# Tails of q and k of two batches: two transfers over 128 partitions in place of four over 64, turned by matmuls with every second identity group, and another set of planning constants

## Chip, core, metric

One core of a Trainium2 chip runs the whole program. The metric is device time in microseconds, the median of several executions. A profile is one further execution, with its own time.

## What is computed

Sliding-window attention for 8 batches of 8 heads, 576 tokens, head dimension 64 (a token attends to keys at most 32 positions away), and behind it a two-layer feed-forward net on the 4608 tokens. Inputs and output are float32; the kernel multiplies in bfloat16.

```python
scores = scale * np.matmul(q, k.transpose(0, 1, 3, 2))        # window = 32
scores = np.where(np.abs(pos[:, None] - pos[None, :]) <= window, scores, -1e9)
attn   = softmax(scores)
attn_out = np.matmul(attn, v)
x = attn_out.transpose(0, 2, 1, 3).reshape(B * S, H * D)      # 4608 x 512
r = np.maximum(x @ w_in, 0.0)                                 # 512 -> 2048
out = (s * (r * r) + b) @ w_out                               # 2048 -> 512
```

## The kernel before

**An order written by a planner.** The kernel doesn't issue its instructions in program order. It collects tasks (`add`): a stream (TensorE "pe", ScalarE "act", VectorE "dve", GpSimd "pool", and "sp", which issues nearly all DMAs), a few instructions, a cost in ns, what is read and written, and a key. `plan` then simulates the five streams and a DMA queue: of all tasks whose inputs are ready it takes the one that can start first, the key deciding between equals. The order that comes out is fixed in the program; at run time each engine works its list from front to back and waits on semaphores. So a task that is late holds up all that stands behind it in the list of its engine, whatever else is ready. `fill` puts spare matmuls (L563, L564) on constants into gaps of TensorE that the plan expects in the first 26 us.

**Constants at the top** choose, for each kind of task, the engine (`K0`, `Q0`, `K1`, `Q1`: casts of k and q of batches 0 and 1; `WINE`, `WOUTE`: casts of the weights; `EV1`, `EV2`: casts of v; `EARLYP`, `ADDE`, `XTE`), the PSUM bank (`TURN1`, `SCORE1`, `EARLYW`), the order of the loads (`ORDER0`, `ORDER1`), and keys (`LASTK`, `TURNKEY`, `SUMS`, `PREP`, `ADDK`, `HELD`).

**The start** has to bring in 8 MB of weights and the q, k, v of the first batches. SP issues the loads of batch 0 in the order of `ORDER0`: four head pairs of q and k ("p", L724, 256 KB each, 128 partitions with 1 KB of each of two heads), v in two pieces ("r", L685), the first block of w_in ("w", L640, two loads of 512 KB), the tail ("e", L737), three more blocks of w_in and the last unit of v ("v", L668). `ORDER1` does the same for w_out and batch 1. Each load goes into one of 8 staging buffers (`STG`); a cast to bfloat16 by some engine (L643, L757) frees the buffer.

**Body and tail.** 576 tokens are not a multiple of 128. For batches 0 and 1 tokens 0 to 511 of q and k come by head pair, four successive tokens on a partition, and TensorE transposes them (L770; L776 copies from PSUM into `QT` and `KT`). The tail, tokens 512 to 575 of all eight heads, is a task of its own. `load_rest` (L732 to L743) issues four transfers of 64 KB, q and k for the even heads onto partitions 0 to 63 and for the odd heads onto 64 to 127: 4 heads times 16 groups of four tokens on 64 partitions, 1 KB each. They go into the second half of a staging buffer whose first half holds a head pair (`HOST`); for batch 1 SP first waits until that pair has landed (`waits=[land["paired", b]]`). One cast (L757, engine `REST[b]`) makes the tail bfloat16, and `turn_rest` (L781 to L798) turns it: for each of the 8 blocks of 64 columns a 64x64 transpose of the upper and one of the lower partitions, 16 in all, written to PSUM as bfloat16 (L788), then one copy each into `QT` and `KT` on engine `TAIL[b]` (L796, L797). `last_scores` (L1045) needs the tail, and behind it stand the last units of the batch.

**After the start.** `joint` does attention times v for two units (L938), `finish` divides (L962, L964) and transposes the result into `XT`: on TensorE (L971, copied by L979) for the first `XPE` units, by DMA transpose (L988) for the others. `s1` is the first layer for four groups of 128 hidden features (L1211, relu L1218, square L1220). `FIRST` gives the order of these for the first three token blocks (224, 128, 160 tokens); a block needs its part of `XT`, and w_in. `early` does the second layer of the first 512 tokens (L1262) two slices of w_out at a time, as they come, in four PSUM banks that `EARLYP` empties (L1274); `added` adds the constant row later (L1284, key `ADDK`), once `colsum` has made it (L1292 to L1316). From batch 2 on q and k are turned by DMA transposes, and first layer, second layer (L1229, written out by L1245 and L1249) and attention alternate on TensorE to the end.

Of the kernel before, what the change touches and what calls it, by code (L numbers as in the profile page):

```python
# [7 lines left out]
BF16 = mybir.dt.bfloat16  # L8
# [9 lines left out]
NPAIR = H // 2  # L18
# [4 lines left out]
VW = 66  # L23
QB = 176
LAG = 1
SPLIT = (1, 3)
WHOLE = 9
SPREAD = ('act', 'dve', 'dve', 'act')
K0 = ('dve', 'act', 'pool', 'dve')
Q0 = ('dve', 'dve', 'dve', 'dve')  # L30
ORDER0 = (('p', 0), ('p', 1), ('p', 2), ('p', 3), ('r', 0), ('r', 1), ('w', 0), ('e', 0), ('w', 1), ('v', 4), ('w', 2), ('w', 3))
RUN = 4
ROWE = ("pool", "dve")
PLACEK = (-26.3, -24.6, -23.5)
PLACEB = ('AVN', 'W', 'W')
BANK0 = ('AVN', 'SC', 'O', 'SC', 'O')
SCORE0 = ('SC', 'O', 'SC', 'O', 'SC')
OPENK = -65
LASTK = -19.3
WINE = ("pool", "pool", "pool", "pool")  # L40
TURNKEY = -19.5
TURN = (None, 0)
FIRST = ((0, 0), (None, 0), (1, 1), (0, 1), (1, 0), (0, 2), (1, 2), (2, 2), (2, 0), (2, 1), (0, 3), (2, 3), (None, 0), (None, 0), (1, 3), (None, 0), (None, 0))
WOUTE = (('dve', 'pool'), ('pool', 'pool'), ('act', 'dve'), ('dve', 'dve'))
TAIL = ('dve', 'act')
HOST = (("k", 3), ("q", 0))
HELD = (2600.0, 1600, 2800, 3600)
OPEN = -19.0
REST = ('pool', 'dve')
ORDER1 = (('w', 0), ('p', 2), ('w', 1), ('p', 1), ('p', 0), ('w', 3), ('w', 2), ('e', 0), ('p', 3), ('v', 2), ('v', 0), ('v', 1), ('v', 3), ('v', 4))  # L50
XTS = 2500
EARLYW = (('W', 0), ('W', 1), ('W', 0), ('AVN', 1), ('W', 1), ('AVN', 1), ('SC', 0), ('O', 0), ('O', 0), ('W', 1), ('AVN', 1), ('W', 1), ('AVN', 1), ('W', 1), ('SC', 0), ('W', 1), ('O', 1), ('W', 1), ('AVN', 0), ('AVN', 0))
SUMS = -20
PREP = -13.5
SUME = 'pool'
SUMC = 'act'
EARLYP = ("act", "act", "act", "act")
ADDE = ('pool', 'dve', 'dve', 'dve')
ADDK = 0
SUMAT = 2  # L60
# [348 lines left out]
def bass_sliding_window_symmetric__then__act_starrelu_kernel(  # L409
# [23 lines left out]
    with ExitStack() as es:  # L433
# [26 lines left out]
        NAT = [NATS[:, i, :] for i in range(NNAT)]  # L460
# [19 lines left out]
        IDENT = sb((128, 128), BF16, "ident")  # L480
# [24 lines left out]
        add = g.add  # L505
# [79 lines left out]
        for p0 in (0, 64):  # L585
# [3 lines left out]
                                                 start=True, stop=True)  # L589
# [30 lines left out]
        land = {}  # L620
# [111 lines left out]
        def load_rest(b, load_key, eng, key, slack):  # L732

            si = land["pair", b, *HOST[b]]
            assert b or ring["stg"] - land["at", b] < NSTG
            stg = STG[si][:, DM:2 * DM]
            add("sp", [lambda e, x=x, p0=p0, src=src: e.dma_start(  # L737
                stg[p0:p0 + 64, 256 * x:256 * x + 256],
                src[b, p0 // 64:H:2, BODY:S, :].rearrange("r (p i) d -> r p (i d)", i=ROWS)) for x, src in enumerate((q, k)) for p0 in (0, 64)],
                2000.0, writes=[("STR", b)], key=load_key, dma=("l", 16, 60.0), waits=[land["paired", b]] if b else [])  # L740
# [40 lines left out]
        def turn_rest(b, key, banks, waits=()):  # L781

            slot = b % 2
            ni, nat = land["rest", b]()
            res, tile = banks[take("bank", len(banks))]
            view = tile.bitcast(BF16)[:, 0:512].rearrange("p (x i a s) -> p x a s i", x=2, i=ROWS, a=NPAIR)
            flat = tile.bitcast(BF16)[:, 0:512]
            add("pe", [lambda e, j=j, p0=p0: e.transpose(flat[p0:p0 + 64, 64 * j:64 * j + 64], nat[p0:p0 + 64, 64 * j:64 * j + 64],  # L788
                                                         IDENT[p0:p0 + 64, p0:p0 + 64]) for j in range(2 * ROWS) for p0 in (0, 64)],
                280.0, form="64", reads=[("NAT", ni), "IDENT"], writes=[res], key=key, waits=waits)  # L790
            last = BODY // 64
            for name, dst, src in (("QT", QT[slot][:, :, WIN + BODY:WIN + S], view[:, 0, :, :, :]),
                                   ("KT", KT[slot][:, :, BODY:S], view[:, 1, :, :, :])):
                dst = dst.rearrange("p a (s i) -> p a s i", i=ROWS)
                eng = TAIL[b]
                add(eng, (lambda e, dst=dst, src=src: e.copy(dst, src)) if eng == "act" else  # L796
                    (lambda e, dst=dst, src=src: e.tensor_copy(dst, src)), {"dve": 155 + 1.04 * 256, "act": 170 + 0.833 * 256}[eng],  # L797
                    reads=[res], writes=[(name, slot, last, pr) for pr in range(NPAIR)], key=key)  # L798
# [207 lines left out]
        def pair_scores(b, pr):  # L1006
# [98 lines left out]
        def attention():  # L1105
# [500 lines left out]
```

## Time and profile before

| | |
|---|---|
| median of 3 runs | 320.65 us (319.98 to 321.68) |
| the profiled execution, whole | 319.61 us |
| its span, first to last instruction | 317.9 us |
| mean granted TensorE clock | 0.989 |
| VectorE, ScalarE, GpSimd busy | 57%, 46%, 37% of the span |
| DMA | 56.24 MB, mean 177 GB/s; in steps of 5 us 248 to 379 GB/s between 5 and 45 us |

How to read what follows: times are microseconds from the start of the span. PE is TensorE's matmuls, PEld its weight loads, DVE VectorE, ACT ScalarE, POOL GpSimd, SPq the queue that issues DMAs. A timeline line gives start, length, engine, source line, operation, output and inputs, a count, and in brackets how long the engine was idle before it and what it waited for. In a table by windows each engine has its busy time in the window; PEclk is the granted clock as a share of full speed, DMA share the mean busy share of 16 DMA engines.

### The profile page before, as it was taken

Reading aid. Unit: us, or ns where it says so; the run is one execution under the profiler, and the core shown is the slowest. Engines: PE = TensorE matmul, PEld = TensorE weight load, DVE = VectorE, ACT = ScalarE, POOL = GpSimd, SP = SyncE. Lnnn points to the kernel's source line nnn. Section 1 sums busy time; section 2 is a strip of 40 time slices with the busy share of each in tenths; the row PEclk is TensorE's granted clock in tenths of the full one; section 3 lists DMA queues with packets and bytes.
Section 4 is the critical chain, followed back from the end, with each engine's and each line's share of the span. In section 5 each row is a group of like instructions: output and inputs, shape, how many; then the busy total and the mean of one; then the engine's idle time right before and its main releaser. Section 6 shows DMA issues by size and latency. Waiting matters only on the chain.

```text
span 317.9 us, 8061 instructions
## 1 busy us (share of the span) xinstructions
PE 305.4 (96%) x3400; PEld 163.0 (51%) x3400; DVE 181.8 (57%) x359; ACT 145.3 (46%) x230; POOL 117.6 (37%) x149
## 2 busy tenths in 40 slices
PE   8979999889999999999999999999999999999996
PEld 3547945466664455444444444444444444444444
DVE  5545857248976867477567836676654453333412
ACT  4635758525552665556136516553544433333300
POOL 4348513647654735565263662366100000000000
PEclk9989999979999999999999999999999999999999
DMA  7999988995898799797979979998522111000022
GB/s 228 358 301 379 326 265 216 224 177 116 283 215 179 209 247 167 199 292 142 172 166 296 179 154 254 271 177 174 122 60 58 50 62 52 33 33 36 34 88 83
DMA packets 99015, 56.24 MB, mean 177 GB/s; under 512 B 70496, under 2 KB 90208, under 8 KB 98976
## 3 DMA queue, kind: packets, MB, share of 16 engines
q1 hardware_dynamic: 98976, 55.69, 72.6%
q8 instruction: 28, 0.46, 0.6%
q14 instruction: 11, 0.09, 0.1%
HBM read 36.70 MB, written 9.44 MB: 145 GB/s over the span
## 4 chain that ended last, share of the span: by engine, by line
PE 82%; DMA 9%; POOL 2%; SPq 2%; issue 1%; DVE 1%; ACT 1%; POOLq 0%
PE w L1211 35%; PE o L1229 35%; DMA stg<-in_k_dram 5%; PE avn L938 4%; DMA stg<-in_q_dram 4%; PE sc L880 2%; PE o L1262 2%; SPq L737 1%; PE avn L1262 1%; PE avn L971 1%; PE avn L1211 1%; ACT outs L1274 1%; POOL outs L1284 1%; PE sc L938 0%; POOL kt L846 0%
## 5 line engine op out<-in xcount | busy, mean ns | idle before, releaser
L1211 PE MATMUL w<-xt,win 128*128 128x512 bf16 (+4 forms) x656 | 135.6, 347 | 0.5 <-ACT r L1218 0.5
L1218 ACT ACTIVATE r<-w 128x512 bf16<-128x512 f32 (+2 forms) x137 | 81.0, 591 | 106.3 <-PE w L1211 96.5
L1229 PE MATMUL o<-wout,gt 128*128 128x512 bf16 (+1 forms) x528 | 124.2, 373 | 0.0
L1220 DVE TENSOR_TENSOR gt<-r 128x512 bf16<-128x512 bf16 (+2 forms) x148 | 78.5, 543 | 79.6 <-ACT r L1218 79.1
L1211 PEld LDWEIGHTS w<-xt,win 128*128 128x128 bf16 x656 | 61.7, 100 | 54.6 <-ACT r L1218 1.9
L1229 PEld LDWEIGHTS o<-wout,gt 128*128 128x128 bf16 x528 | 50.1, 98 | 53.8
L829 POOL CAST nat<-stg 128x1024 bf16<-128x1024 f32 (+1 forms) x36 | 40.8, 1132 | 38.1 <-DMA stg<-in_q_dram 23.8
L846 POOL COPY kt<-ktr 128x512 bf16<-128x512 bf16 (+1 forms) x30 | 32.5, 1084 | 23.3 <-DMA ktr<-nat 21.8
L908 ACT ACTIVATE ex<-sc 128x1024 bf16<-128x1024 f32 (+1 forms) x28 | 28.7, 1024 | 27.0 <-PE avn L938 25.8
L1245 DVE SCALAR_TENSOR_TENSOR outs<-o,sb,cvec 128x512 f32<-128x512 f32 (+1 forms) x33 | 24.1, 730 | 17.5 <-PE o L1229 17.3
L677 POOL CAST vb<-vst 128x512 bf16<-128x512 f32 (+1 forms) x25 | 17.4, 696 | 23.1 <-DMA vst<-in_v_dram 22.5
L912 DVE TENSOR_TENSOR ex<-ex,mask 128x1024 bf16<-128x1024 bf16 (+1 forms) x28 | 22.1, 789 | 2.2 <-ACT ex L908 1.6
L964 DVE TENSOR_TENSOR xn<-avn,rec 128x512 bf16<-128x512 f32 (+1 forms) x30 | 20.6, 688 | 0.8
L938 PE MATMUL avn<-vb,ex 64*64 64x65 bf16 x912 | 19.2, 197 | 0.4 <-POOL kt L846 0.2
L938 PEld LDWEIGHTS avn<-vb,ex 64*64 64x64 bf16 x912 | 12.5, 106 | 13.1 <-issue 8.5
L880 PE MATMUL sc<-qt,kt 64*64 64x128 bf16 x432 | 11.4, 216 | 0.0
L962 DVE RECIPROCAL rec<-avn 128x8 f32<-128x8 f32 (+1 forms) x30 | 6.0, 201 | 8.8 <-PE avn L938 7.7
L643 POOL CAST win<-stg 128x1024 bf16<-128x1024 f32 x8 | 8.5, 1066 | 4.4 <-DMA stg<-in_moe_w_in_dram 4.3
L1262 PE MATMUL o<-wout,gt 128*128 128x512 bf16 x32 | 8.9, 381 | 0.0
L1262 PE MATMUL avn<-wout,gt 128*128 128x512 bf16 x32 | 8.7, 379 | 0.0
L757 DVE CAST nat<-stg 128x512 bf16<-128x512 f32 x12 | 5.5, 468 | 4.9 <-DMA stg<-in_k_dram 2.8
L880 PEld LDWEIGHTS sc<-qt,kt 64*64 64x64 bf16 x432 | 7.5, 107 | 0.0
(156 smaller groups left out, 181.4 us busy)
## 6 DMA issues: line engine op xcount, KB each, us to landing
out_dram<-outs SPq DMA_DIRECT2D x35, 256.0 KB, 2.4
vst<-in_v_dram SPq DMA_DIRECT2D x28, 256.0 KB, 5.6
stg<-in_k_dram SPq DMA_DIRECT2D x6, 1024.0 KB, 10.9
stg<-in_q_dram SPq DMA_DIRECT2D x6, 1024.0 KB, 6.0
stg<-in_moe_w_in_dram SPq DMA_DIRECT2D x8, 512.0 KB, 10.4
stg<-in_moe_w_out_dram SPq DMA_DIRECT2D x8, 512.0 KB, 8.1
stg<-in_q_dram SPq DMA_DIRECT2D x8, 256.0 KB, 6.1
stg<-in_k_dram SPq DMA_DIRECT2D x8, 256.0 KB, 5.5
```

The source lines that it names most:

```text
L829: add(eng, lambda e, x=x: e.tensor_copy(nat[0:top, 1024 * x:1024 * x + 1024].rearrange("p (i h d) -> p h i d", h=H, i=2), stg[0:top, :].re ...
L846: add("pool", lambda e, c=c, w=w: e.tensor_copy(KT[slot][:, :, c:c + w].rearrange("p a (s i) -> p a s i", i=4), KTR[slot][:, :, :, c // 4: ...
L880: fns = [lambda e, pr=pr, x=x, b=b, j=j, hp=hp: e.matmul(SC[64 * x:64 * x + 64, hp, pr * 128:pr * 128 + 128], lhsT=KT[b % 2][64 * hp:64 * ...
L908: add("act", lambda e, dst=flat_dst, src=flat_src: e.activation(dst, src, AF.Exp, bias=0.0, scale=0.125), 170 + 0.833 * 512 * len(hs), rea ...
L912: add("dve", lambda e, flat=flat, mask=mask: e.tensor_tensor(flat, flat, mask, ALU.mult), 155 + 0.53 * 512 * len(hs), form="two", reads=[( ...
L938: return [lambda e: e.matmul(av[64 * x:64 * x + 64, h, 0:D + 1], lhsT=buf[64 * g:64 * g + 64, h % 2, h // 2, c:c + 64], rhs=VB[64 * g:64 * ...
L1211: add("pe", [lambda e, g=g, kc=kc: e.matmul(wt[:, g, :], lhsT=WIN_BF[:, kc, (f0 + g) * 128:(f0 + g + 1) * 128], rhs=XT[:, kc, t0 % XR:t0 % ...
L1218: add("act", lambda e: e.activation(rt, wt, AF.Relu, bias=0.0, scale=1.0), 170 + 0.833 * ng * nt, reads=[(name, wb)], writes=[("R1", rb)], ...
L1220: add("dve", lambda e: e.tensor_tensor(GT[gs][:, f0:f0 + ng, g0:g0 + nt], rt, rt, ALU.mult), 155 + 0.53 * ng * nt, form="two", reads=[("R1 ...
L1229: add("pe", [lambda e, fc=fc: e.matmul(O[:, ob, 0:cn], lhsT=GT[gs][:, fc, g0:g0 + 128], rhs=WOUT_BF[:, fc, c0:c0 + cn], start=(fc == 0), s ...
L1245: add("dve", lambda e: e.scalar_tensor_tensor(OUTS[us][:, 0:cn], bank, SB128[:, 0:1], CVEC[:, c0:c0 + cn], ALU.mult, ALU.add), 210 + 1.05 ...
L1262: add("pe", [lambda e, fc=fc, bank=bank, gs=gs, g0=g0: e.matmul(bank, lhsT=GT[gs][:, fc, g0:g0 + 128], rhs=WOUT_BF[:, fc, :], start=(fc == ...
```

## The change

The loads: two transfers, of 128 KB, each over all 128 partitions, heads in order, in place of four.

```diff
-            add("sp", [lambda e, x=x, p0=p0, src=src: e.dma_start(
-                stg[p0:p0 + 64, 256 * x:256 * x + 256],
-                src[b, p0 // 64:H:2, BODY:S, :].rearrange("r (p i) d -> r p (i d)", i=ROWS)) for x, src in enumerate((q, k)) for p0 in (0, 64)],
-                2000.0, writes=[("STR", b)], key=load_key, dma=("l", 16, 60.0), waits=[land["paired", b]] if b else [])
+            add("sp", [lambda e, x=x, src=src: e.dma_start(
+                stg[:, 256 * x:256 * x + 256],
+                src[b, :, BODY:S, :].rearrange("h (p i) d -> h p (i d)", i=ROWS)) for x, src in enumerate((q, k))],
+                1200.0, writes=[("STR", b)], key=load_key, dma=("l", 16, 50.0), waits=[land["paired", b]] if b else [])
```

Now even and odd heads alternate on the partitions, 16 by 16. The turning therefore becomes 16 plain matmuls: the weights are a block of 64 columns over all 128 partitions, the moving operand the 64 columns of the identity that belong to the even heads (result on PSUM partitions 0 to 63) or to the odd ones (64 to 127). The result is float32 in PSUM. The task loses the mark `form="64"`.

```diff
-            view = tile.bitcast(BF16)[:, 0:512].rearrange("p (x i a s) -> p x a s i", x=2, i=ROWS, a=NPAIR)
-            flat = tile.bitcast(BF16)[:, 0:512]
-            add("pe", [lambda e, j=j, p0=p0: e.transpose(flat[p0:p0 + 64, 64 * j:64 * j + 64], nat[p0:p0 + 64, 64 * j:64 * j + 64],
-                                                         IDENT[p0:p0 + 64, p0:p0 + 64]) for j in range(2 * ROWS) for p0 in (0, 64)],
-                280.0, form="64", reads=[("NAT", ni), "IDENT"], writes=[res], key=key, waits=waits)
+            view = tile.rearrange("p (x i a s) -> p x a s i", x=2, i=ROWS, a=NPAIR)
+            heads = IDENT.rearrange("p (a two s) -> p two a s", a=NPAIR, two=2)
+            add("pe", [lambda e, j=j, p0=p0: e.matmul(
+                tile[p0:p0 + 64, 64 * j:64 * j + 64].rearrange("p (a s) -> p a s", a=NPAIR), lhsT=nat[:, 64 * j:64 * j + 64],
+                rhs=heads[:, p0 // 64, :, :], start=True, stop=True, skip_group_check=True)
+                for j in range(2 * ROWS) for p0 in (0, 64)],
+                480.0, reads=[("NAT", ni), "IDENT"], writes=[res], key=key, waits=waits)
```

And constants, most of them:

```diff
-SPLIT = (1, 3)
+SPLIT = (4, 3)
-K0 = ('dve', 'act', 'pool', 'dve')
-Q0 = ('dve', 'dve', 'dve', 'dve')
-ORDER0 = (('p', 0), ('p', 1), ('p', 2), ('p', 3), ('r', 0), ('r', 1), ('w', 0), ('e', 0), ('w', 1), ('v', 4), ('w', 2), ('w', 3))
+K0 = ('dve', 'dve', 'pool', 'pool')
+Q0 = ('dve', 'dve', 'act', 'dve')
+ORDER0 = (('p', 0), ('p', 1), ('p', 2), ('p', 3), ('r', 0), ('r', 1), ('w', 0), ('v', 4), ('e', 0), ('w', 1), ('w', 2), ('w', 3))
-LASTK = -19.3
-WINE = ("pool", "pool", "pool", "pool")
+LASTK = -21.3
+WINE = ('dve', 'act', 'pool', 'pool')
-WOUTE = (('dve', 'pool'), ('pool', 'pool'), ('act', 'dve'), ('dve', 'dve'))
+WOUTE = (('act', 'pool'), ('act', 'pool'), ('act', 'dve'), ('pool', 'dve'))
-REST = ('pool', 'dve')
-ORDER1 = (('w', 0), ('p', 2), ('w', 1), ('p', 1), ('p', 0), ('w', 3), ('w', 2), ('e', 0), ('p', 3), ('v', 2), ('v', 0), ('v', 1), ('v', 3), ('v', 4))
+REST = ('dve', 'dve')
+ORDER1 = (('w', 0), ('w', 1), ('p', 2), ('p', 1), ('p', 0), ('w', 3), ('w', 2), ('e', 0), ('p', 3), ('v', 2), ('v', 4), ('v', 3), ('v', 0), ('v', 1))
-PREP = -13.5
-SUME = 'pool'
-SUMC = 'act'
-EARLYP = ("act", "act", "act", "act")
+PREP = -17.5
+SUME = 'act'
+SUMC = 'dve'
+EARLYP = ('act', 'dve', 'dve', 'act')
-ADDK = 0
-SUMAT = 2
+ADDK = 11.0
+SUMAT = 3
-XPE = 19
+XPE = 20
-EV1 = ('dve', 'pool', 'pool', 'pool', 'dve')
-EV2 = ('pool', 'pool', 'dve', 'pool', 'pool')
+EV1 = ('pool', 'dve', 'pool', 'pool', 'dve')
+EV2 = ('pool', 'pool', 'pool', 'dve', 'dve')
-TURN1 = (1, 0, 3, 1, 0, 3, 0, 0, 1)
-SCORE1 = ('W', 'SC', 'SC', 'W')
+TURN1 = (1, 0, 3, 1, 2, 3, 0, 2, 1)
+SCORE1 = ('SC', 'SC', 'SC', 'W')
-Q1 = ('dve', 'act', 'pool', 'dve')
+Q1 = ('pool', 'pool', 'pool', 'dve')
```

`SPREAD`, `PLACEK`, `OPENK`, `TURNKEY`, `OPEN`, `FIRST`, `HELD`, `SLACK`, `EV0`, `COPYQ` and `XTE` change in an entry or by a few units of a key. The code of the planner is the same before and after.

More of the change, by code (lines that the diff above doesn't have):

```diff
@@ L25 @@
 LAG = 1
-SPLIT = (1, 3)
+SPLIT = (4, 3)
 WHOLE = 9
-SPREAD = ('act', 'dve', 'dve', 'act')
-K0 = ('dve', 'act', 'pool', 'dve')
-Q0 = ('dve', 'dve', 'dve', 'dve')
-ORDER0 = (('p', 0), ('p', 1), ('p', 2), ('p', 3), ('r', 0), ('r', 1), ('w', 0), ('e', 0), ('w', 1), ('v', 4), ('w', 2), ('w', 3))
+SPREAD = ('act', 'dve', 'act', 'act')
+K0 = ('dve', 'dve', 'pool', 'pool')
+Q0 = ('dve', 'dve', 'act', 'dve')
+ORDER0 = (('p', 0), ('p', 1), ('p', 2), ('p', 3), ('r', 0), ('r', 1), ('w', 0), ('v', 4), ('e', 0), ('w', 1), ('w', 2), ('w', 3))
 RUN = 4
 ROWE = ("pool", "dve")
-PLACEK = (-26.3, -24.6, -23.5)
+PLACEK = (-28.3, -27.4, -24.3)
 PLACEB = ('AVN', 'W', 'W')
@@ L37 @@
 SCORE0 = ('SC', 'O', 'SC', 'O', 'SC')
-OPENK = -65
-LASTK = -19.3
-WINE = ("pool", "pool", "pool", "pool")
-TURNKEY = -19.5
+OPENK = -55
+LASTK = -21.3
+WINE = ('dve', 'act', 'pool', 'pool')
+TURNKEY = -18.5
 TURN = (None, 0)
-FIRST = ((0, 0), (None, 0), (1, 1), (0, 1), (1, 0), (0, 2), (1, 2), (2, 2), (2, 0), (2, 1), (0, 3), (2, 3), (None, 0), (None, 0), (1, 3), (None, 0), (None, 0))
-WOUTE = (('dve', 'pool'), ('pool', 'pool'), ('act', 'dve'), ('dve', 'dve'))
+FIRST = ((0, 0), (None, 0), (1, 1), (0, 1), (1, 0), (0, 2), (1, 2), (2, 0), (2, 1), (2, 2), (0, 3), (2, 3), (None, 0), (None, 0), (None, 0), (1, 3), (None, 0))
+WOUTE = (('act', 'pool'), ('act', 'pool'), ('act', 'dve'), ('pool', 'dve'))
 TAIL = ('dve', 'act')
 HOST = (("k", 3), ("q", 0))
-HELD = (2600.0, 1600, 2800, 3600)
-OPEN = -19.0
-REST = ('pool', 'dve')
-ORDER1 = (('w', 0), ('p', 2), ('w', 1), ('p', 1), ('p', 0), ('w', 3), ('w', 2), ('e', 0), ('p', 3), ('v', 2), ('v', 0), ('v', 1), ('v', 3), ('v', 4))
+HELD = (3400.0, 1200, 2800, 4000)
+OPEN = -19.25
+REST = ('dve', 'dve')
+ORDER1 = (('w', 0), ('w', 1), ('p', 2), ('p', 1), ('p', 0), ('w', 3), ('w', 2), ('e', 0), ('p', 3), ('v', 2), ('v', 4), ('v', 3), ('v', 0), ('v', 1))
 XTS = 2500
```

8 lines of the change are left out of this document (4 added, 4 removed).

## The prediction

> **What bounds the kernel now.** I read the page's slices first, then TensorE's waits, then the windows around them, then the chain of waits.
>
> ```profile
> PE 305.4 (96%) x3400; PEld 163.0 (51%) x3400; DVE 181.8 (57%) x359; ACT 145.3 (46%) x230; POOL 117.6 (37%) x149
> PEclk9989999979999999999999999999999999999999
> PE w L788 <- POOL nat L757: 2.1, 1, 2.1
> PE sc L938 <- issue: 1.5, 1, 1.5
> PE w L770 <- DVE nat L757: 1.4, 1, 1.4
> PE o L938 <- ACT xt L979: 0.8, 1, 0.8
> PE o L1211 <- ACT xt L979: 0.6, 1, 0.6
> ```
>
> TensorE is busy for 305.4 of 317.9 us. Its waits are few, and they lie in the first 80 us; so do the two dips of the clock (third and ninth slice, of 8 us each). From 80 us on TensorE is full. Whatever the change does is won or lost in the start, or is work added to a full TensorE. Windows of 1 and 5 us (TensorE's busy time first, then PEld, DVE, ACT, POOL, clock, DMA share, GB/s):
>
> ```profile
> 18.00:19.00 1.00, 0.30 (x16) 0.18 (x16) 0.61 (x2) 0.27 (x1) 0.00 (x0) 1.00 1.18 231
> 19.00:20.00 1.00, 0.00 (x0) 0.00 (x0) 0.28 (x1) 0.00 (x0) 0.25 (x1) 1.00 1.09 248
> 20.00:25.00 5.00, 4.58 (x50) 3.34 (x54) 1.15 (x3) 1.68 (x4) 3.42 (x7) 0.66 1.05 367
> ...
> 47.00:48.00 1.00, 0.00 (x0) 0.00 (x0) 0.09 (x1) 0.09 (x1) 0.00 (x0) 1.00 1.04 248
> 48.00:49.00 1.00, 0.61 (x6) 0.44 (x7) 0.76 (x3) 0.70 (x2) 0.00 (x0) 1.00 0.31 69
> ```
>
> The 2.1 us wait, for the cast of batch 0's tail, is followed by a clock of 0.66 on the mean of 20 to 25 us: 5 x 0.34 = 1.7 us more. The 1.4 us wait at 47 us leaves the clock at 1.00. The chain of waits (start, length, what) names what both hang on:
>
> ```profile
> 9.83 9.81 DMA stg<-in_k_dram
> 19.75 0.63 POOL nat L757
> 20.42 0.44 PE w L788 x16
> ...
> 40.56 7.33 DMA stg<-in_k_dram
> 47.91 0.44 DVE nat L757
> 48.39 0.40 PE w L770 x4
> ```
>
> The first DMA is the last of the four tail transfers of batch 0, 9.81 us from issue to landing; the second is the head pair of batch 1 that SP issues right behind the tail of batch 1. So the start is bound by a saturated DMA queue, and both of TensorE's waits on it are behind a tail.
>
> **The loads.** How long a tail occupies the queue is read from the casts that wait for landings (GpSimd at first, VectorE later; a bracket that names a DMA means that the cast began when the load had landed):
>
> ```profile
> 14.10 1.04 POOL L643 CAST win<-stg 128x1024 bf16<-128x1024 f32 x1 [1.79 <-DMA stg<-in_moe_w_in_dram]
> 15.69 1.04 POOL L643 CAST win<-stg 128x1024 bf16<-128x1024 f32 x1 [0.54 <-DMA stg<-in_moe_w_in_dram]
> 19.75 0.62 POOL L757 CAST nat<-stg 128x512 bf16<-128x512 f32 x1 [3.02 <-DMA stg<-in_k_dram]
> ...
> 44.38 0.69 DVE L643 CAST wout<-stg 128x1024 bf16<-128x1024 f32 x1 [1.26 <-DMA stg<-in_moe_w_out_dram]
> 47.91 0.43 DVE L757 CAST nat<-stg 128x512 bf16<-128x512 f32 x1 [2.23 <-DMA stg<-in_k_dram]
> 48.57 0.76 DVE L757 CAST nat<-stg 128x512 bf16<-128x512 f32 x2 [0.24 <-DMA stg<-in_q_dram]
> ```
>
> Two w_in loads of 512 KB land 15.69 - 14.10 = 1.59 us apart; by bytes, 256 KB cost 0.80 us. The tail of batch 0 (256 KB) lands 19.75 - 15.69 = 4.06 us behind the load before it. In batch 1 the k of the pair lands 47.91 - 44.38 = 3.53 us behind the last w_out load, with the tail between them; the pair's q follows after 0.66 us, so the tail takes 3.53 - 0.66 = 2.87 us. Each of the eight transfers of 64 KB thus takes 0.7 to 1.0 us, as long as 256 KB over 128 partitions. Time doesn't go with bytes, and in those microseconds the queue moves less (231 and 248 GB/s against 367 above).
>
> What a transfer of 128 KB over 128 partitions takes, no row shows. Bounds: as long as two of the old ones, since it has as many rows of 1 KB (gain 0); or as long as its bytes ask for (gain 4.06 - 0.80 + 2.87 - 0.66 = 5.47 us). I take the time of one old transfer, as the rows show a time that hangs on the transfer and little on its bytes. Batch 0: 4.06 / 2 = 2.03 us won. Batch 1: 2.87 / 2 = 1.44. Together **-3.47 us** on the landing of the last pair. What lies between the tails (w_in, w_out, pairs) comes 2.03 us earlier, as the DMA share stays near 1.
>
> The Trainium skill has two rules here, in "DMA: Bandwidth & Descriptors". "Rules for kernel authors" advises one transfer for two partition halves, but says that both halves spray over all 16 engines anyway; by it merging saves no transfer time, which the 4.06 us for 256 KB speak against. "Why a DMA increments its semaphore by 16 and not by 1" says that the engines used are the largest number up to 16 that divides the outermost dimension of source and destination: 4 before (4 heads, 64 partitions), 8 after (8 heads, 128 partitions), which would give the sum the same half.
>
> On SP:
>
> ```profile
> 7.89 1.32 SPq L737 DMA_DIRECT2D stg<-in_q_dram  x2
> 9.25 1.11 SPq L737 DMA_DIRECT2D stg<-in_k_dram  x2
> ...
> 38.21 1.16 SPq L737 DMA_DIRECT2D stg<-in_q_dram  x2
> 39.41 1.10 SPq L737 DMA_DIRECT2D stg<-in_k_dram  x2
> 40.56 0.46 SPq L724 DMA_DIRECT2D stg<-in_k_dram  x1
> ```
>
> Four issues take 2.5 and 2.3 us of SP, two will take half. I count nothing for it: the loads behind wait in the queue for 7 us and more (the chain). Without that cover it would be worth 1.2 us a tail. The v unit now issued ahead of the first tail (128 KB) moves the tail back by 0.4 us by bytes, and is out of the queue behind it; nothing in sum.
>
> **Can TensorE follow?** It must lose 3.47 us before the last pair. It has 2.1 + 0.6 + 1.4 us of waits and 1.7 us of clock there, 5.8 us. So the DMA queue stays the bound, and what is left over stays a wait.
>
> **The turning.**
>
> ```profile
> 20.42 0.44 PE L788 MATMUL w<-ident,nat 64*64 64x64 bf16 x16 [2.12 <-POOL nat L757]
> 9.20 0.33 PE L563 MATMUL avn<-onesw 128*128 128x128 bf16 x3
> 20.90 0.42 DVE L797 COPY qt<-w 128x256 bf16<-128x256 bf16 x1 [1.61 <-PE w L788]
> 13.34 0.42 DVE L716 CAST vb<-avn 128x256 bf16<-128x256 f32 x1
> ```
>
> 16 transposes take 0.44 us, two side by side. [...] Three matmuls of 128 columns take 0.33 with 0.22 of it the first, so 0.055 each; 16 of these would take 0.22 + 15 x 0.055 = 1.05. The new ones move 64 columns, so they lie between 0.44 and 1.05; I take +0.2 a batch, nearer to the first, whose operand and count they have: **+0.4 us**, bounds 0 to +1.2, both on the path. Reading float32 from PSUM costs VectorE the same 0.42 us for 128x256, so the copies cost nothing more.
>
> **XPE 19 to 20** puts four more transposes on a TensorE that is full there: 4 x 0.055 = **+0.2 us**. The DMA transposes that they replace had no one waiting on the chain.
>
> **The other constants** move casts and copies between engines with idle time and shift keys. I put them at nothing: the cover is DVE at 57%, ACT at 46%, POOL at 37%. If it is gone, what is late next is seen between 60 and 80 us:
>
> ```profile
> 60.12 1.85 ACT outs L1274 x3
> 63.36 1.51 issue
> ...
> 60.00:70.00 10.00, 7.59 (x133) 5.27 (x135) 3.87 (x8) 4.64 (x9) 5.03 (x6) 0.83 1.08 147
> ```
>
> Here 0.8 us (ACT empties four banks, then copies `XT`) and 1.5 us (nothing that the profile shows) come with 10 x 0.17 = 1.7 us of lost clock: 4.0 us that can go or double.
>
> **The sum.** -3.47 + 0.4 + 0.2 = -2.87 us. Against the profiled execution's 319.61 that is 316.7; it lies 1.04 under the median of 320.65, so on the scale of the runs **317.8 us**. With the bounds of the loads and the turning: 320.65 - 5.47 + 0.2 = 315.4 to 320.65 + 1.2 + 0.2 = 322.0.
>
> **Rivals.**
>
> *More is won.* `EARLYP` gives two of the four banks to VectorE, so the 0.8 us wait at 62 us goes. The 1.5 us alone would be like the 1.4 us at 47 us, which cost no clock; then the 1.7 us go too. 317.8 - 0.8 - 1.7 = 315.3 us. For it: three pieces of ACT on the chain just there. Against it: VectorE has its own chain (L962, L964) there.
>
> *The tails take as long as before.* Same rows of 1 KB, same bytes: 320.65 + 0.6 = 321.3 us. For it: the queue serves rows, not transfers. Against it: the pair transfers have rows of 1 KB too, and 256 of them take 0.66 us.
>
> *VectorE becomes the bound.* `ADDK` lets the four additions of the constant row give way to other work until some 11 us later, into a stretch where VectorE is full:
>
> ```profile
> 75.75 3.85 DVE L1284 TENSOR_TENSOR outs<-outs,cvec 128x512 f32<-128x512 f32 x3 [0.15 <-ACT cvec L1316]
> 80.00:90.00 10.00, 10.00 (x144) 7.16 (x141) 9.92 (x17) 5.54 (x9) 6.92 (x7) 1.00 0.94 293
> ```
>
> 9.92 of 10 us are taken there, so 3.85 us more would hold up the squares (L1220) and `XT`, and TensorE with them. It decides once TensorE's wait is nearer to the 2.1 us that cost clock than to the 1.4 that didn't: then 3.85 + 1.7 us of clock, 317.8 + 5.5 = 323.3 us. Against it: the additions leave 75 to 80 us, so VectorE comes to this stretch with less behind it. The Trainium skill ("TensorE: Matmul & The Clock Gate", Part 1) lets the clock fall after an idle window of some 3.4 us; by it the 2.1 us wait would have cost no clock, and this rival would be 323.3 - 1.7 = 321.6. The trace shows the drop behind 2.1 us.
>
> **How the numbers follow.** Forecast 0.46 (own range 316.2 to 319.2), more won 0.22, tails as before 0.15, VectorE 0.17. The measurement tells 0.5% from no change: below 319.05 is faster, above 322.25 slower. Faster: 0.46 + 0.22 = 0.68. Same: 0.15. Slower: 0.17. The range runs from 314.6, under the case of more won, to 321.7, over that of unchanged tails; it leaves out the VectorE case and the edge of the first.
>
> **What would show it.** The queue: the cast of batch 0's tail begins near 17.7 us (19.75 - 2.03) and the last pair's k is cast near 44.5 us (47.91 - 3.47). Only two issues of L737 a batch. TensorE's wait before the turning is gone or under 0.5 us, and the clock stays at 1.00 between 21 and 25 us. The 16 matmuls take 0.5 to 0.8 us. It is wrong if the tail's landing hasn't moved, if a wait of 2 us or more stands elsewhere before 100 us, or if TensorE is below 98% busy from 85 us on.

## The result, and the profile after

| | changed kernel | before, same chip |
|---|---|---|
| median | 318.12 us (316.62 to 319.41, 12 runs) | 321.19 us (318.9 to 323.49, 12 runs) |
| ratio | 0.9904, 95% interval 0.9874 to 0.9934 | |
| profiled execution, whole (span; mean clock) | 319.02 us (317.3; 0.989) | 319.61 us (317.9; 0.989) |

The change wins 321.19 - 318.12 = 3.07 us. The two profiled executions lie only 0.6 us apart: the one of after is 0.90 us above its median, the one of before 1.58 us below. So the profiles show where the work has moved, and the sizes are taken from the runs.

The clock over the span (page, 40 slices of 7.9 us) and TensorE's longest waits (line, releaser, us in total, times, longest), after:

```profile
PEclk9989997999999999999999999999999999999999
```

```profile
PE o L770 <- POOL nat L757: 2.4, 1, 2.4
PE o L1231 <- issue: 2.1, 13, 0.2
PE w L770 <- DVE nat L757: 1.3, 1, 1.3
PE avn L973 <- DVE xn L966: 1.3, 2, 0.9
```

The waits of 2.1 us ahead of the tail's turning and of 1.5 us at 63 us are gone from the list. (The 13 short gaps at L1231 are matmuls whose records are missing: 3356 matmuls are recorded for 3396 weight loads.) But a wait of 2.4 us stands in batch 1, near 47 us, where it was 1.4. The windows, after (columns as in the prediction):

```profile
15.00:20.00 5.00, 3.93 (x90) 1.97 (x86) 3.31 (x9) 2.23 (x7) 0.00 (x0) 1.00 1.09 280
20.00:25.00 5.00, 4.87 (x83) 3.29 (x80) 1.82 (x5) 3.64 (x5) 0.89 (x4) 0.66 1.05 387
45.00:50.00 5.00, 2.59 (x21) 1.67 (x20) 3.45 (x8) 2.39 (x5) 1.92 (x3) 0.86 0.83 168
50.00:55.00 5.00, 4.84 (x59) 2.11 (x58) 1.61 (x5) 3.50 (x6) 1.21 (x2) 0.80 1.08 324
```

The clock still falls behind 20 us, as before, and now also between 45 and 55 us (5 x 0.14 + 5 x 0.20 = 1.7 us); the fall between 65 and 70 us is gone. The casts and the turning, after:

```profile
17.37 0.69 DVE L643 CAST win<-stg 128x1024 bf16<-128x1024 f32 x1 [1.62 <-DMA stg<-in_moe_w_in_dram]
19.56 0.43 DVE L757 CAST nat<-stg 128x512 bf16<-128x512 f32 x1
44.04 0.69 DVE L643 CAST wout<-stg 128x1024 bf16<-128x1024 f32 x1 [0.80 <-DMA stg<-in_moe_w_out_dram]
46.83 0.43 DVE L757 CAST nat<-stg 128x512 bf16<-128x512 f32 x1 [1.13 <-DMA stg<-in_k_dram]
46.86 0.87 POOL L757 CAST nat<-stg 128x512 bf16<-128x512 f32 x1 [3.79 <-DMA stg<-in_k_dram]
47.67 0.76 DVE L757 CAST nat<-stg 128x512 bf16<-128x512 f32 x2 [0.41 <-DMA stg<-in_q_dram]
47.79 0.40 PE L770 MATMUL o<-ident,nat 128*128 128x128 bf16 x4 [2.39 <-POOL nat L757]
```

The cast of batch 0's tail has no bracket: VectorE was busy with L966 until then, so it tells only that the tail had landed by 19.56. The k of the last pair is cast at 46.83 in place of 47.91, 1.08 us earlier, not 3.47. Batch 1's tail, read as in the prediction: 46.83 - 44.04 - (47.67 - 46.83) = 1.95 us, before 2.87.

The turn at 47.79 is not that of the last pair. It is that of an earlier pair of batch 1, cast by GpSimd at 46.86, and this cast too begins with the landing of the last pair's k. That is a flaw in the order of tasks of both kernels: all loads of batch 1 are added (`add`) ahead of their casts, so a load that reuses one of the 8 staging buffers waits only until the earlier load has landed, not until its cast has read it. In the kernel before SP issues the last pair's k at 40.56, as soon as the q of an earlier pair has landed in the same buffer, and the cast of that q runs at 47.91 on ScalarE, behind the landing of the k. Some casts of batch 1 thus read the later load's data and wait for a landing that they would not need. It is the same before and after, so the times compare like with like; no run is without it.

**Lost clock time.** Each run is listed with its span and its mean granted clock. Span x (1 - clock) is the time that TensorE's clock lost; the rest is what the span would be at full clock. Means here and below are taken over the runs within 1.5% of the kernel's fastest, as slower ones are a state that any kernel shows: before 3.79 us lost and 314.7 left (28 runs beside the first four experiments), after 1.43 lost and 315.0 left (12 runs). The lost time falls by 2.4 us, most of the gain, and the rest doesn't move as far as such means can tell (0.2 us, give or take 0.7). This has to be explained beside the loads.

### The profile page after: what moved, and what is told of

Same layout as the page of the kernel before. It is cut to its first block, busy times and chain, and to the rows that moved or that the text cites. A ratio compares the mean times of both kernels' runs of the same rounds, so it can differ in the third digit from the quotient of the medians.

```text
span 317.3 us, 7989 instructions
## 1 busy us (share of the span) xinstructions
PE 300.5 (95%) x3356; PEld 162.5 (51%) x3396; DVE 184.4 (58%) x364; ACT 147.5 (46%) x230; POOL 109.5 (35%) x142
## 4 chain that ended last, share of the span: by engine, by line
PE 84%; DMA 9%; issue 2%; DVE 2%; ACT 1%; SPq 1%; POOL 0%
PE w L1213 36%; PE o L1231 34%; DMA stg<-in_k_dram 4%; PE avn L940 4%; DMA stg<-in_moe_w_in_dram 3%; PE o L1264 2%; PE sc L882 2%; DMA stg<-in_q_dram 2%; PE avn L1264 1%; PE avn L973 1%; ACT r L1220 1%; DVE xn L966 1%; PE avn L1213 1%; PE o L940 1%; PE sc L940 0%
## 5 line engine op out<-in xcount | busy, mean ns | idle before, releaser
L1213 PE MATMUL w<-xt,win 128*128 128x512 bf16 (+4 forms) x642 | 131.9, 342 | 2.3 <-ACT r L1220 1.3
L1231 PE MATMUL o<-wout,gt 128*128 128x512 bf16 (+1 forms) x507 | 121.0, 372 | 2.4 <-issue 2.1
L1213 PEld LDWEIGHTS w<-xt,win 128*128 128x128 bf16 x656 | 60.6, 98 | 53.4 <-ACT r L1220 1.3
L1231 PEld LDWEIGHTS o<-wout,gt 128*128 128x128 bf16 x528 | 50.2, 98 | 53.5
L848 POOL COPY kt<-ktr 128x512 bf16<-128x512 bf16 (+1 forms) x30 | 31.2, 1041 | 17.9 <-DMA ktr<-nat 16.5
L966 DVE TENSOR_TENSOR xn<-avn,rec 128x512 bf16<-128x512 f32 (+1 forms) x30 | 20.6, 688 | 0.8
L940 PE MATMUL avn<-vb,ex 64*64 64x65 bf16 x912 | 19.2, 197 | 0.1
L940 PEld LDWEIGHTS avn<-vb,ex 64*64 64x64 bf16 x912 | 12.5, 106 | 13.0 <-issue 10.2
L677 POOL CAST vb<-vst 128x512 bf16<-128x512 f32 x21 | 15.0, 714 | 9.9 <-DMA vst<-in_v_dram 9.1
L757 POOL CAST nat<-stg 128x512 bf16<-128x512 f32 x6 | 4.2, 699 | 12.9 <-DMA stg<-in_k_dram 8.6
L1264 PE MATMUL o<-wout,gt 128*128 128x512 bf16 x29 | 7.3, 380 | 0.5 <-issue 0.5
```

What stands on the lines that cost most here:

```text
L848: add("pool", lambda e, c=c, w=w: e.tensor_copy(KT[slot][:, :, c:c + w].rearrange("p a (s i) -> p a s i", i=4), KTR[slot][:, :, :, c // 4: ...
L940: return [lambda e: e.matmul(av[64 * x:64 * x + 64, h, 0:D + 1], lhsT=buf[64 * g:64 * g + 64, h % 2, h // 2, c:c + 64], rhs=VB[64 * g:64 * ...
L966: add("dve", lambda e: e.tensor_tensor(XN[xi][0:p1, :].rearrange("p (a c) -> p a c", a=H), av[0:p1, :, 0:D], REC[ri][0:p1, :].rearrange("p ...
L1213: add("pe", [lambda e, g=g, kc=kc: e.matmul(wt[:, g, :], lhsT=WIN_BF[:, kc, (f0 + g) * 128:(f0 + g + 1) * 128], rhs=XT[:, kc, t0 % XR:t0 % ...
L1231: add("pe", [lambda e, fc=fc: e.matmul(O[:, ob, 0:cn], lhsT=GT[gs][:, fc, g0:g0 + 128], rhs=WOUT_BF[:, fc, c0:c0 + cn], start=(fc == 0), s ...
L1264: add("pe", [lambda e, fc=fc, bank=bank, gs=gs, g0=g0: e.matmul(bank, lhsT=GT[gs][:, fc, g0:g0 + 128], rhs=WOUT_BF[:, fc, :], start=(fc == ...
```

## The experiments

All ratios are against runs of the kernel before on the same chip. "Lost" and "rest" are computed as above.

| run | median us | ratio (95%) | lost us | rest us |
|---|---|---|---|---|
| e1_tails_only | 317.87 | 0.9919 (0.9885 to 0.9953) | 1.66 | 314.5 |
| e2_constants_only | 320.70 | 1.0008 (0.9976 to 1.0040) | 3.88 | 315.0 |
| e3_after_16 | 318.17 | 0.9928 (0.9898 to 0.9959) | 1.43 | 315.1 |
| e4_before_16 | 317.25 | 0.9894 (0.9855 to 0.9933) | 1.49 | 314.0 |
| e5_tail0 | 319.47 | 0.9988 (0.9947 to 1.0029) | 2.55 | 315.4 |
| e6_tail1 | 319.79 | 0.9982 (0.9946 to 1.0017) | 1.86 | 315.8 |
| e7_before_warm | 319.99 | 0.9997 (0.9957 to 1.0037) | 2.55 | 315.7 |
| e8_after_warm | 318.60 | 0.9955 (0.9922 to 0.9989) | 1.80 | 315.1 |
| e9_before_short | 318.39 | 0.9912 (0.9877 to 0.9947) | 1.90 | 314.5 |
| e10_tails_short | 316.32 | 0.9856 (0.9802 to 0.9910) | 0.00 | 314.3 |
| e11_16_short | 314.53 | 0.9810 (0.9763 to 0.9857) | 0.00 | 313.0 |
| e12_short_refilled | 320.26 | 0.9993 (0.9952 to 1.0034) | 1.98 | 316.6 |

The kernel before on the four chips used: lost 3.79, 3.30, 3.93, 3.87; rest 314.7, 315.0, 315.2, 315.1.

In the traces every fall of the clock before 310 us is a stretch of 3.41 us (in two traces two in a row) at half the full clock, so one fall costs some 1.7 us. The kernels' traces have none (e3, e10 to e12) to two (before, after, e2, e5, e7) of them.

### Tails or constants

e1 is the kernel before with the two new hunks of the diff (loads and turning of both tails) and the old constants; e2 is the changed kernel with the old hunks and the new constants. The costs that the planner sees stay those of the kernel that is edited, so that its order stays.

> The new loads and turning of both tails in the order, constants and planning costs of before, so that every engine's list is the old one. Theory T (the gain comes from the shorter stay of the tails in the DMA queue): the tail of batch 0 is cast near 18 us instead of 19.75, the last pair of batch 1 near 45 to 46 us instead of 47.9, and the time falls by 1.5 to 3 us, ratio 0.990 to 0.995. Theory C (the gain comes from the other order of work, above all from the stalls between 60 and 70 us): ratio 0.997 to 1.002, and TensorE only waits longer elsewhere. Both: the 16 matmuls take 0.44 us as the 16 transposes did.

> The new constants and the order that the planner made for the changed kernel, with the four transfers and the 64x64 transposes of before. Theory T: the gain is gone, ratio 0.998 to 1.004; with the v unit of 128 KB issued ahead of it the tail of batch 0 is cast later than in before, near 21 to 22 us. Theory C: ratio 0.988 to 0.994, as the whole change.

The tails alone give the whole gain, the constants nothing. The stay of the tails in the queue in e1:

```profile
15.78 1.04 POOL L643 CAST win<-stg 128x1024 bf16<-128x1024 f32 x1 [0.62 <-DMA stg<-in_moe_w_in_dram]
19.39 0.44 PE L788 MATMUL w<-ident,nat 128*64 128x64 bf16 x16 [0.16 <-POOL nat L757]
20.46 1.04 POOL L643 CAST win<-stg 128x1024 bf16<-128x1024 f32 x1 [1.12 <-DMA stg<-in_moe_w_in_dram]
44.09 0.69 DVE L643 CAST wout<-stg 128x1024 bf16<-128x1024 f32 x1 [1.65 <-DMA stg<-in_moe_w_out_dram]
46.34 0.43 DVE L757 CAST nat<-stg 128x512 bf16<-128x512 f32 x1 [0.96 <-DMA stg<-in_k_dram]
47.07 1.65 DVE L757 CAST nat<-stg 128x512 bf16<-128x512 f32 x3 [0.30 <-DMA stg<-in_q_dram]
```

and its chain of waits (start, length, what):

```profile
18.72 0.62 POOL nat L757
...
20.95 8.63 DMA stg<-in_moe_w_out_dram
29.61 0.90 DVE wout L643
30.53 7.01 DMA stg<-in_q_dram
37.56 0.64 SPq L737
```

Batch 0: 18.72 - 15.78 = 2.94 us (before 4.06); batch 1: 46.34 - 44.09 - (47.07 - 46.34) = 1.52 (before 2.87). So the tails stay 1.12 and 1.35 us less. But the next w_in load comes only 0.70 us earlier than in the kernel before, whose cast of it is

```profile
21.16 1.04 POOL L643 CAST win<-stg 128x1024 bf16<-128x1024 f32 x1 [0.79 <-DMA stg<-in_moe_w_in_dram]
```

and the last w_out load ahead of the second tail is cast at 44.09, against 44.38, 0.29 us. Part of the 1.12 us is gone at once, and the traces say why: a tail doesn't hold the whole queue. The semaphore of a w_in load rises in 16 steps while it lands, that of a tail transfer in 4 in the kernel before and in 8 in e1. In the kernel before 12 of the next w_in load's 16 steps had come by 18.03 us, while the tail was still landing (19.64), and the last four came at 20.73 to 21.11; in e1 8 had come by 17.45 and the other 8 by 20.40. Read as one step for each of the 16 DMA engines, a tail holds 4 (or 8) of them for a long time, and the others meanwhile go on with the loads behind it. What is left shrinks further, from 0.70 us at this load to 0.42 at the first w_out load's landing and 0.29 at the last; in the chain of before the same stretch goes by way of

```profile
30.39 0.60 DVE wout L643
31.02 7.18 DMA stg<-in_q_dram
```

so that this cast, which frees a staging buffer for a later load, ends 0.48 us earlier in e1 (30.51 and 30.99). No run isolates what takes away the rest.

TensorE's waits in e1 and in e2:

```profile
PE sc L940 <- issue: 2.5, 1, 2.5
PE w L770 <- DVE nat L757: 1.1, 1, 1.1
PE w L788 <- POOL nat L757: 0.2, 1, 0.2
```

```profile
PE o L770 <- POOL nat L757: 4.0, 1, 4.0
PE w L788 <- DVE nat L757: 1.4, 1, 1.4
```

In e1 the wait at the turning is gone, and the one for nothing that the profile shows has grown from 1.5 to 2.5 us. In e2 that one is gone, and a pair of batch 1 waits 4.0 us (for GpSimd's cast, as in after): what the constants take away at 63 us they give back at 45.

### Sixteen groups in place of eight heads

The tail is laid out with partition = 8 x group + head:

```diff
-                src[b, :, BODY:S, :].rearrange("h (p i) d -> h p (i d)", i=ROWS)) for x, src in enumerate((q, k))],
+                src[b, :, BODY:S, :].rearrange("h (p i) d -> p h (i d)", i=ROWS)) for x, src in enumerate((q, k))],
...
-            heads = IDENT.rearrange("p (a two s) -> p two a s", a=NPAIR, two=2)
+            heads = IDENT.rearrange("p (s a two) -> p two a s", a=NPAIR, two=2)
```

> The changed kernel with the tail's rows dealt out differently: partition 8 p + h instead of 16 h + p, so that the outermost dimension of the source counts 16 groups of tokens and not 8 heads; the turning takes every second column of the identity instead of every second group of 16. Same bytes, rows of 1 KB, transfers, matmuls and order. Theory T, if the time of a tail hangs on over how many DMA engines its outermost dimension is dealt: the last pair lands another 0.5 to 1.5 us earlier, ratio to before 0.984 to 0.989. If rows of 1 KB or the number of transfers set it: 0.990, as the changed kernel.

> The same 16 p-groups layout of the tail in the order and constants of before. Theory T with the outermost dimension: another 0.5 to 1.5 us less than the new loads alone in that order, ratio 0.986 to 0.992, the last pair of batch 1 near 44.5 to 45.5 us. With transfers or rows as the cause: the same as the new loads alone. Theory C: 0.997 to 1.002.

In e4 the tail of batch 0 takes 2.23 us and the last pair's k is cast at 45.23 (e1: 2.94 and 46.34). Same rows of 1 KB, same bytes, same partitions and number of transfers in e1 and e4: the stay hangs on the outermost dimension, 8 or 16. The step from 4 (4.06 us) to 8 also halves the number of transfers, so it doesn't isolate this. Each figure is of one trace, and in batch 0 the stays of other traces overlap (old loads 2.37 to 4.26 us, new ones 2.22 to 3.26); in batch 1 they don't: 2.71 to 3.30 us with 4, 0.99 to 1.95 with 8, 0.59 to 0.87 with 16. By the intervals, neither e3 nor e4 can be told from its version with 8; e3's interval excludes the 0.984 to 0.989 that theory T named for it, and e4's 0.9894 lies in what T named.

### One tail alone, and waits filled with work

e5 and e6 use the new loads and turning for one batch only (`if b == 0:`, `if b == 1:`). e7 and e8 put spare matmuls of 128x512 into a wait, nothing else:

```diff
+            t = _Task(len(g.tasks), "pe", [four] * n, 216.0 * n, 0.0, task.key, None, 0.0, [], None)
...
+            g.order.insert(g.order.index(task), t)
...
+        warm(*land["rested", 0], 9)
```

> The kernel before with the new loads and the new turning for batch 0's tail alone. Theory Q (the landing itself carries the gain through to the end): the queue is 1.1 us earlier here (2.94 in place of 4.06 us in the run with both tails), and TensorE's 2.1 us wait at 18 us is gone: ratio near 0.9965, most of the gain only with batch 1's tail. Theory K (TensorE gets the same work done at full clock in the same time in any case; what is saved is a clock drop, about 1.7 us each, behind a wait of about 2 us): this tail alone takes away the wait that lies ahead of the drop of 20 to 25 us, so ratio 0.994 to 0.997, the mean granted clock of the runs up by 0.003 to 0.006, and span x clock unchanged near 315 us.

> The kernel before with the new loads and the new turning for batch 1's tail alone. Theory Q: the last head pair lands 1.35 us earlier (1.52 in place of 2.87 us): ratio near 0.9958. Theory K: the 1.4 us wait at 47 us in the kernel before cost no clock, and the 2.1 us wait at 18 us with its drop stays: ratio 0.998 to 1.002, mean granted clock as before (0.987).

> The kernel before, loads and turning of the tails unchanged, with 9 spare matmuls of 128x512 (about 1.9 us) on TensorE just ahead of the turning of batch 0's tail, in the wait of 2.1 us. Theory Q: no load comes earlier, so ratio 0.998 to 1.002. Theory K: the tail is cast as late as before (near 19.7 us), but the clock stays at 1.00 between 20 and 25 us: ratio 0.9945 to 0.9965, mean clock up by 0.003 to 0.006.

> The changed kernel with 8 spare matmuls of 128x512 (about 1.7 us) on TensorE ahead of the turn that waits 2.4 us at 45 to 48 us. Theory Q: as the changed kernel (0.990) or slower. Theory K: the dips of the clock between 45 and 55 us (0.86 and 0.80 in the profile of after) go, ratio 0.986 to 0.989, mean granted clock 0.997 or more.

By the medians neither theory holds in all four; by the intervals only K's forecast for e8 (0.986 to 0.989) is excluded. One tail alone gives nothing that can be told from zero (nor, by the intervals, from half of the 0.8% that both gave). e7 removes the wait at 18 us and keeps the clock at 1.00 there, without any gain; its clock falls later, as its windows show:

```profile
20.00:25.00 5.00, 4.81 (x70) 3.65 (x69) 1.15 (x3) 2.11 (x5) 3.17 (x7) 1.00 1.06 358
50.00:55.00 5.00, 4.84 (x54) 2.46 (x57) 1.80 (x4) 2.73 (x6) 1.47 (x2) 0.69 1.03 257
65.00:70.00 5.00, 3.84 (x33) 2.96 (x34) 1.96 (x5) 0.85 (x2) 2.32 (x4) 0.67 1.11 139
```

e8 fills the wait of 2.4 us near 47 us, with the clock at 1.00 from 45 to 55, and is, if anything, slower than the changed kernel. What else changes is seen in the last of four groups of 16 matmuls of the attention units (L938, L940 or L943), in the kernel before, in e7 and in e8 (timeline of TensorE alone):

```profile
62.38 0.32 PE L938 MATMUL o<-vb,ex 64*64 64x65 bf16 x16 [0.81 <-ACT xt L979]
...
63.07 0.29 PE L938 MATMUL sc<-vb,ex 64*64 64x65 bf16 x13
64.86 0.22 PE L938 MATMUL sc<-vb,ex 64*64 64x65 bf16 x3 [1.51 <-issue]
```

```profile
64.66 0.20 PE L940 MATMUL sc<-vb,ex 64*64 64x65 bf16 x4
66.16 0.29 PE L940 MATMUL sc<-vb,ex 64*64 64x65 bf16 x12 [1.30 <-issue]
```

```profile
63.62 0.23 PE L943 MATMUL sc<-vb,ex 64*64 64x65 bf16 x7
65.46 0.28 PE L943 MATMUL sc<-vb,ex 64*64 64x65 bf16 x9 [1.61 <-issue]
```

The wait splits a task of 16 matmuls in the middle, and with 9 matmuls more ahead of it the break comes exactly 9 earlier (13 becomes 4). It belongs to a number of instructions, not to the work.

### The break between blocks of instructions

```diff
-            t = _Task(len(self.tasks), "pe", [n.spare[2]] * (count // 4) + [n.spare[1]] * (count % 4), each * count, 0.0, b.key, None, 0.0, [], None)
+            t = _Task(len(self.tasks), "pe", [n.spare[2]] * max(1, count // 4), each * count, 0.0, b.key, None, 0.0, [], None)
```

This is e9 (on the kernel before), e10 (on e1) and e11 (on e4): the planner's spare matmuls in the first 26 us become 14 where they were 32. e12 is e9 with 18 spare matmuls of 128 columns ahead of the turning, inserted as in e7.

> The kernel before, tails unchanged, with 18 fewer instructions pairs in TensorE's list ahead of 60 us: each group of spare matmuls in the first 26 us keeps its matmuls of 512 columns and loses those of 128 (at least one of 512 stays). Theory F (the 1.5 us in which TensorE waits for nothing that the profile shows, near 63 us, is a wait for its own instructions, which come in blocks of a fixed number through the full DMA queue; the runs with 9 and 8 spare matmuls had the break 9 and 8 matmuls earlier): the break moves 18 matmuls back, into matmuls of 256 columns that take about 0.19 us each, so TensorE gets there some 2.8 us later and the block has come: no wait over 0.3 us in the attention units at 62 to 65 us, clock above 0.95 from 65 to 70 us, ratio 0.990 to 0.995. Theory N (the break belongs to the place in the attention units, to their data or their bank): the wait stays after the 13th matmul of the fourth unit, ratio 0.998 to 1.002.

> The kernel before with the new loads and turning of both tails and nothing else (as in the run with tails only, 0.9919 there), and the same 18 fewer spare matmuls. Theory F: the wait of 2.5 us at 62 to 64 us in the run with tails only, in which the earlier landing was lost again, is gone or under 0.5 us, the clock stays above 0.95 from 65 to 70 us, ratio 0.982 to 0.988. Theory N: the wait stays, ratio 0.990 to 0.994.

> The kernel before with the tails laid out for partition = 8 x group + head (0.9894 in its own run) and the same 18 fewer spare matmuls. Theory F: ratio 0.980 to 0.987, below the changed kernel's 0.9904. Theory N: ratio 0.987 to 0.991.

> The kernel before, tails unchanged, with the 18 fewer spare matmuls of the run that measured 0.9912, and 18 other spare matmuls of 128 columns (about 1.0 us) put just ahead of the turning of batch 0's tail, in a wait of 2.5 us there. From the turning on each instruction of TensorE has the place in the count that it has in the kernel before. Theory F (the gain of the shorter list comes from where the breaks between the blocks of instructions fall): the break is back after the 13th matmul of the fourth attention unit near 63 us, with a wait of 1 to 2.7 us, and the gain goes: ratio 0.997 to 1.002. Theory W (the shape of the early spare matmuls, fewer and longer, made the gain by itself): ratio 0.989 to 0.994 wherever the break is.

The break in e9, e10 and e12:

```profile
65.03 1.81 PE L1211 MATMUL w<-xt,win 128*128 128x256 bf16 x15
68.71 0.28 PE L1211 MATMUL w<-xt,win 128*128 128x256 bf16 x1 [1.87 <-issue]
```

```profile
62.42 1.81 PE L1213 MATMUL w<-xt,win 128*128 128x256 bf16 x15
65.24 0.28 PE L1213 MATMUL w<-xt,win 128*128 128x256 bf16 x1 [1.01 <-issue]
```

```profile
63.51 0.28 PE L940 MATMUL sc<-vb,ex 64*64 64x65 bf16 x13
65.61 0.22 PE L940 MATMUL sc<-vb,ex 64*64 64x65 bf16 x3 [1.82 <-issue]
```

With 18 matmuls fewer the break comes 18 matmuls later (3 and 15), with 18 put back it is where it was, and the gain of e9 is gone: 0.9912 becomes 0.9993. So theory F holds in the place of the break and in the times, and theory W falls with them. F was wrong in one point: it expected the wait to vanish. In e9 it is 1.87 us, no shorter than before. What is gone is lost clock time (3.93 to 1.90 us). A reading that fits, argued and not isolated by a run: in the kernel before, TensorE does nothing between 61.57 and 64.86 us but 61 small matmuls of 65 columns, and the clock falls behind it at 65.7; in e9 15 matmuls over the full array lie ahead of the break, and it doesn't. But in e12 the time comes back as rest (316.6) and not as lost clock time (1.98). So what the break costs is shown by the times; how it comes to cost them stays open.

The page counts the transfers that bring instructions, q8, beside the data's q1 (transfers, MB, share of 16 engines), before:

```profile
q1 hardware_dynamic: 98976, 55.69, 72.6%
q8 instruction: 28, 0.46, 0.6%
```

0.46 MB in 28 transfers are 16.4 KB each. In the trace's records of q8 and of TensorE's own instructions, the sixth transfer lands, and the wait at the break ends, in every kernel with a wait there (us):

```
                     block starts   lands   wait ends   lag
before                   61.85      63.33     64.86     1.53
e1_tails_only            61.24      62.92     64.30     1.38
e4_before_16             59.83      61.15     62.66     1.51
e5_tail0                 62.59      63.85     65.11     1.26
e6_tail1                 61.39      62.76     64.12     1.36
e7_before_warm           63.62      64.82     66.16     1.34
e8_after_warm            63.05      64.09     65.46     1.37
e9_before_short          66.04      67.32     68.71     1.39
e10_tails_short          62.06      63.66     65.23     1.57
e11_16_short             62.08      63.12     64.46     1.34
e12_short_refilled       62.82      64.35     65.61     1.26
```

The wait ends 1.3 to 1.6 us behind the landing. In after the block lands at 63.32 and TensorE reaches the place at 66.06, so no wait; in e2 it lands 3.6 us ahead. In e1 TensorE reaches the place at 61.57, 1.56 us earlier than before (63.13), and the block lands only 0.41 us earlier: its wait grows by 1.0 us. This loss doesn't show in the times, though. In the old order the tails gave 320.97 - 317.87 = 3.10 us (e1), with the break moved, from e9 to e10 on one chip, 318.39 - 316.32 = 2.07, and by the intervals the two can't be told apart.

e11 is faster than both kernels: 0.981 against the changed kernel's 0.9904, in intervals that don't meet, and in its six runs no clock is lost at all.

## Why the prediction came out, step by step

The predicted 317.8 us, 2.85 under the median it started from, stands against a measured gain of 3.07 (by the interval 2.1 to 4.0). The cause was right: e1 has the gain, e2 has none. The way from the cause to the end was not as predicted, and that the total came so near is luck in part: the landing of the last pair was to bring 3.47 us and brought 1.08 in after, and the turning was to cost 0.4 and cost nothing.

- **The loads.** Batch 1's tail was right in e1, 1.35 us won for 1.44; in after, 0.92. Batch 0's was too large by these two traces, 1.12 for 2.03: a transfer of 128 KB took more than one of 64 KB (2.94 / 2 = 1.47 us against 4.06 / 4 = 1.02). With the spread of batch 0's stays from trace to trace, the size is uncertain.
- **"What lies between the tails comes 2.03 us earlier."** This step failed. It read a tail's stay as time of the whole queue, but the next w_in load lands in e1 only 0.70 us earlier, since most of its steps come while the tail is still landing, and 0.29 us were left at the last w_out load. The last pair's landing moved by 1.57 us in e1 and by 1.08 in after, not 3.47.
- **"What is left over stays a wait."** True of e1, but the waits moved and were not only removed: 2.1 to 0.2 us ahead of the turning, 1.4 to 1.1 at 47 us, 1.5 to 2.5 at 63 us. The sum counted landings and left the clock as it was; in the runs most of the gain is clock (3.79 to 1.43 us lost). The total agrees with the forecast, and its parts do not. How earlier landings become less lost clock, no run isolates.
- **The 1.5 us that nothing showed** was put down as able to go or to double. It went in after and in e2 and grew to 2.5 in e1 and 2.7 in e5, and it is the wait for a block of instructions (e7, e9, e12).
- **The turning** cost 0.44 us as transposes and 0.44 as matmuls; the +0.4 was 0. The four transposes of XPE can't be told apart from the rest.
- **The other constants at nothing**: 1.0008 in e2. Their cover was not idle engines but a trade: no wait at 63 us, but 4.0 us near 47 us with the old tails, 2.4 with the new.
- **SP**: in after two issues took 1.96 and 1.31 us in place of 2.5 and 2.3. The chain of e1 runs through the second tail's issues (37.56), but the load behind them is in the queue for another 7.4 us. What SP's time is worth, no run shows.
- **Rivals.** *The tails take as long as before* fell with e1. *VectorE becomes the bound* did not occur:

```profile
80.00:90.00 10.00, 9.89 (x151) 6.85 (x153) 8.26 (x18) 5.84 (x9) 4.50 (x4) 1.00 1.04 304
```

 VectorE has 8.26 of 10 us there (before 9.92), since the additions still ran ahead of 80 us. *More is won* had its stretch right (60 to 70 us in after, with both waits gone and the clock at 1.00), but not what would come in its place at 45.
- **The signs named.** In e1: the turning waits 0.2 us, the clock is 1.00 behind 20 us, two issues a batch, 0.44 us for 16 matmuls (0.5 was the lower bound). In after: the clock at 20 to 25 us is still 0.66, and a wait of 2.4 us stands near 47 us, one of the things said to make the prediction wrong. From 85 us on TensorE's recorded busy time is 97.8%, under the 98% named, but with 2.9 us of gaps that are missing records; without them it is 99.1%. Its time was right nonetheless.
- **"The trace shows the drop behind 2.1 us."** The rule drawn from this row does not carry. In e12 TensorE waits 2.35 us, and the clock stays; its timeline and its windows:

```profile
48.84 0.40 PE L770 MATMUL w<-ident,nat 128*128 128x128 bf16 x4 [2.35 <-DVE nat L757]
```

```profile
45.00:50.00 5.00, 2.65 (x25) 1.55 (x24) 2.06 (x6) 1.86 (x4) 0.17 (x1) 1.00 0.64 152
50.00:55.00 5.00, 5.00 (x68) 2.43 (x65) 3.46 (x7) 4.35 (x7) 1.89 (x3) 1.00 0.99 237
```

 The Trainium skill ("TensorE: Matmul & The Clock Gate", Part 1) has the clock halved after an idle window of 3413 ns that runs free of the program. With it agree the size of a fall (stretches of 3.41 us at half clock in the traces, 1.7 us each) and that like waits cost clock in one run and not in the next. In the traces a stretch need not be idle throughout: in the kernel before TensorE waits 2.1 of the 3.41 us ahead of the first fall, and the measurement decides. The falls of a trace lie multiples of 3.41 us apart. Cut into such stretches, the 14 traces have ten in which TensorE is busy under 0.40 of the time, and all ten were followed by the half clock; the next, with e12's wait in it (0.42), was not. But four more falls stand behind stretches busy at 0.51 to 0.83 and filled with small matmuls, so busy time alone doesn't decide.

## What to carry to other kernels

Earlier data is worth only what the next limit lets through: before counting it at the end, look for what is late next, here TensorE's own instructions behind the same full DMA queue; and ask whether a slow transfer holds the whole queue or a part of its engines, as here. A wait that splits a task in the middle, with nothing named as its cause, is to be tested by adding a few instructions far ahead: if the break moves by as many, it is the block of instructions, and fewer and longer instructions, or a place where TensorE has long matmuls, move it away. Where a kernel's runs differ in mean clock, compute the lost clock time for each run before explaining a difference of two medians from one pair of profiles.

## What was not expected of the hardware

- TensorE's instructions come in blocks of 16.4 KB through DMA, and while the loads fill the engines a block took 1.0 to 1.7 us and was usable only 1.3 to 1.6 us after it landed. The break stands behind 1729 recorded instructions of TensorE (matmuls and weight loads) in the traces of before and e9 to e12, and behind 1724 in those that lack a few records. e3, e5 and e8 have an earlier one behind 449 (in e8 at 20.43 us, 0.84 us), 1729 - 449 = 1280 instructions ahead. The Trainium skill ("Runtime: NRT & Kernel Launch", "Instruction fetch mechanics") has blocks of 256 instructions, of which 1280 is a multiple, and calls the crossing mostly hidden; waits of 0.9 to 2.7 us at the break in eleven of these fourteen kernels show that it is not hidden here.
- The stay of one and the same 256 KB in the queue: in batch 1 2.71 to 3.30 us with an outermost dimension of 4 (four transfers), 0.99 to 1.95 with 8 and 0.59 to 0.87 with 16 (two transfers each). The landing comes in 4, 8 or 16 steps a transfer, and other loads go on meanwhile.
- Between the kernel before and after, the lost clock time was the main difference (3.79 and 1.43 us), while the rest stayed within 0.3. Over all kernels the rest lay between 314.0 and 315.8 us but for e11 (313.0) and e12 (316.6).
